# A fused adaLN, linear attention and gated MLP kernel: LayerNorm 1 transposes all on TensorE, query weights read transposed from DRAM, first key products in halves, and a new order of instructions

## The chip, the cores and the metric

The kernel runs on one core of a Trainium2 chip. The core has five engines with instruction queues of their own: TensorE (PE; its weight loads are listed as PEld), VectorE (DVE), ScalarE (ACT), GpSimd (POOL) and SyncE (SP), which here only issues DMAs. The metric is the time of one execution on the device in microseconds; three executions are known. A profiled execution gives times of single instructions, counted from the first one (the span).

## The reference

One token block of S = 2048 rows with D = 512, H = 32 heads of 16, F = 1376, in bfloat16. Cut to what matters:

```python
mod = (silu(c) @ w_mod)                      # six vectors sa, ca, ga, sb, cb, gb of 512
h = layernorm(x) * (1 + ca) + sa
q, k, v = heads(h @ wqkv)
pq, pk = q @ w_phi, k @ w_phi                # per head, 16 x 16
phi_q = concat(softmax(pq), softmax(-pq));   phi_k = concat(softmax(pk), softmax(-pk))
kv = phi_k.T @ v;  z = phi_k.sum(tokens)     # sums over all 2048 tokens
o = (phi_q @ kv) / (phi_q @ z + 1e-6)
x = x + ga * (o @ wo)
h = layernorm(x) * (1 + cb) + sb
x = x + gb * ((sigmoid(h @ w_gate) * (h @ w_up)) @ w_down)
```

The sums kv and z run over all tokens, so no token can pass the attention before all keys and values have been worked off.

## The kernel before

**Tiles.** The 2048 rows are 16 tiles of 128. `x_sb` holds them with rows on partitions. LayerNorm 1 works per tile: `st1` (statistics, DVE), `rs1` (one over the deviation, on ACT or POOL), `nmr1` (DVE), `xn1` (normalised rows, on POOL, ACT or, for tile 0, DVE). Then the rows must become columns, `h1T`, for the products. The groups `LG` are tiles 0, 1, 2-3, 4-5, ... 14-15. For a group with `TD` 0, PE transposes 128 x 128 blocks into a PSUM bank (`tph`, L841) and ACT or DVE applies the modulation on the way out (`hm1`, L848, L850). For groups 6 and 7 (tiles 10 to 13) `TD` is 1: SP issues a DMA transpose per tile straight into `h1T` (`xT1`, L833), and `hm1` changes `h1T` in place on ACT, DVE or POOL.

**Weights.** The head map `w_phi` is folded into the key and query weights: `bd` is its block-diagonal form, the weights are transposed (keys: `tpw` on PE and `wTc` copies; queries: `wqT`, DMA transposes from `wqk_sb` behind the load `wq0`, L769), multiplied (`fold`, L776) and copied to `wqk_f` (`foldc`, L782, L784). The modulation vectors are products of `wmod_sb` with silu(c), of one column each: `modc1` (LayerNorm 1; its two halves are the two halves of the contraction, loaded by `ld_wm00` and `ld_wm01`, L667), `modca` (ga) and `modc2` (the rest, in halves `modc2.0` and `modc2.1`), L735.

**Keys and values, per tile t.** `K` (four matmuls into `k_ps`, L867), `e` (exponentials of both signs, ACT, L883), `n` (sums, DVE, L886), `r` (reciprocal, DVE, or logarithm and exponential on ACT), `phi` (product, POOL or DVE, L889), `V` and its copy `va` (L907), and `kv` (eight matmuls per tile into two accumulating banks `kvacc`, L280). Tiles 11 and 13 to 15 do `e` to `kv` in parts (`NPART`). After the last tile, `kvm` masks the sums (DVE, L301), `kvp` permutes them (PE with `bdp`, which POOL's `perm` makes, L290, L293) and `kvz` and `kvn` write `kvbd`.

**Queries and the rest.** `Q` (L945) and `qe` (exponentials, L950) work on blocks of 128 features by 512 tokens, 16 in all. Behind `kvp` come, per unit of one or two tiles, `sm` or `num` (products with `kvbd`), divisions `den` and `u`, `o` and its transposition `oT`, `out` (with `wo`, which POOL and DVE scale by ga), `x1`, LayerNorm 2, and per chunk (1, 1, 2, 4, 4, 4 tiles) the MLP: `g`, `u`, the tanh `tg` on ACT, `hm`, `y` (L612), the addition `fin` (L619) and the store `st` (L621). The last tile's `y` is made in 384 and 128 columns.

**What sets the order.** Every step is a task with a name, the engines that it may run on, the keys that it reads and writes, and the buffers that it uses. The text `ORDER` lists all tasks; `arrange` walks it, takes the engine that a suffix names (`@A`, `@D`, `@P`) or else the first of the task's list, and gives buffers out first come, first served. Each engine executes its tasks in that order and waits where data or a buffer is not there. `warm` matmuls have no result that is used.

Of the kernel before, what the change touches and what calls it, by code (L numbers as in the profile page):

```python
# [49 lines left out]
K13 kv8.0 va10 e13.4 r11.2 ld_wu0 e13.0 phi9.0 n13.4 r11.4 r13.4 n13.0 e12.0 phi10.0 K15 Q11 ld_wd kv9.0 V14 phi11.0@D n12.0 e15.4 r13.0@A K14 kv10.0 phi11.2  # L50
phi11.4 phi11.6 e15.0 va13 Q03 Q01 e14.4 r12.0@A va14 e14.0 phi13.4@D phi13.0 phi12.0 n14.4 n14.0 r14.4@A r14.0 n15.0 n15.4 r15.4 phi14.4@D V12 kv11.4 Q13
modc2.0 va12 qe01 phi14.0 phi15.4@D qe13 r15.0@A kv11.0 kv11.6 kv11.2 gra kv12.0 V15 Q02 kv13.4 va15 qe03 phi15.0@D kv14.4 kv13.0 kv15.4 kv14.0 kvm1 kv15.0
Q32 kvm0 qe02 perm kvp2 kvp1 kvp0 kvz2 kvz1 kvz0 kvn0 modc2.1 sm0 sm2 qe32 modc2c kvn2@A kvn1@A wo2 smS2 smS0@D den0 den2 Q12 Q31 qe31 wo3 num00 qe11 num30
num01 Q30 num31 u00 u01 Q23 num20 u30 u31 qe12 u20 tpo0 num21 u21 oT0 wo1 wo0 wo_all sm1 smS1 o3 sm4 smS4 num10 out0 num11 den1 x1_0 qe30 qe23 Q33 Q21 Q22
num61 qe33 u11 st2_0 u10 o2 tpo1 rs2_0 gwb nmr2_0 den4 num70 u70 qe21 oT1 num71 xn2_0 u71 grb wd0 qe22 Q20 out1 wd10 xnT0 num60 x1_1 mod00 mod01 wd4 wd5 wd1
mod03 u60 qe20 mod02@A oT2 oT3 tsw u61 st2_1 out3 out2 u0.10 g0.10 tg0.10 u0.9 g0.9 tg0.9 g0.3 g0.0 wmod_free o7 hm0.10 oT7 hm0.9 wd2 rs2_1 g0.4 u0.0 o6 wd7
wr g0.6 tg0.0 tg0.4 x1_3 u0.4 hm0.0 hm0.4 oT6 nmr2_1 g0.2 u0.6 u0.3 u0.2 u0.8 tg0.6 tg0.3 g0.8 xn2_1 hm0.6 x1_2 sm3 hm0.3 tg0.2 tg0.8 xnT1 hm0.2 g0.1 hm0.8
mod13 mod12@A mod10@A tg0.1 st2_3 g0.7 u0.7 u0.1 tg0.7 mod11@A wd6 smS3 hm0.7 hm0.1 out7 g1.5 u0.5 g1.2 g0.5 tg1.2 tg0.5 u1.2 x1_7 g1.0 u1.5 g1.8 st2_2 hm0.5
hm1.2 g1.9 u1.10 u1.0 rs2_2 tg1.5 tg1.0 hm1.5 hm1.0 g1.10 u1.8 nmr2_2 tg1.10 tg1.8 hm1.10 hm1.8 u1.3 g1.1 g1.3 wd8 xn2_3@P wd3 u1.1 out6 xn2_2 tg1.1 tg1.3
den3 hm1.1 hm1.3 g1.4 g1.7 u1.4 y0.0 tg1.4 wd9 x1_6 hm1.4 y0.1 y0.2 g1.6 tg1.6 num40 y1.0 y0.3 u1.6 num50 y1.1 u1.9 tg1.9 st2_7 st2_6 rs2_4 hm1.6 xnT3 xnT2  # L60
y1.2 y1.3 num51 y0.4 tg1.7 num41 num81 hm1.9 u50 u40 u41 z81 num80 y0.5 y1.4 u1.7 hm1.7 u51 mod22@A z80 mod20@A mod23@P mod21@P num82 y1.5 y0.6 y0.7 nmr2_4
z82@D g2.2 o5 tg2.2 num90 y1.6 y1.7 y0.8 o4 xn2_7@P dn8 u800 u820 y0.9 y0.10 g2.1 tg2.1 y1.8 y1.9 u2.1 g2.4 u2.2 fin0 u811 hm2.2 u821 o8 oT5 oT4 g2.10 y1.10
u2.10 num92 num91 hm2.1 fin1 z91@D tg2.10 tg2.4 u2.4 hm2.10 hm2.4 z90 xn2_6 out4 g2.8 z92 tg2.8 dn9 st0 u2.0 u2.8 g2.5 x1_4 u921 u911 hm2.8 out5 u900 u920
x1_5 u2.5 num100 oT8 z100 tg2.5 o9 hm2.5 st2_4 g2.7 g2.0 tg2.7 xnT7 tg2.0 hm2.0 st2_5 u2.3 g2.3 xnT6 out8 u2.9 u2.7 rs2_3 tg2.3 hm2.3 x1_8 hm2.7 nmr2_3 st2_8
xn2_5@P oT9 g2.6 g2.9 tg2.6 tg2.9 num102 y3.0 u2.6 y3.1 y3.2 num101 y3.3 y3.4 y3.5 num111 hm2.9 z101@D hm2.6 y3.6 mod42@A y3.7 y3.8 y3.9 z102 dn10 y3.10 fin3
xn2_4@P u1000 y2.0 y2.1 y2.2 out9 mod41@P num110 y2.3 x1_9 u1021 z110@D st2_9 xnT5 xnT4 y2.4 st3 y2.5 mod40@A y2.6 y2.7 y2.8 mod31@P mod43@A z111 mod33@P
# [1067 lines left out]
```

## Time and profile before

| | us |
|---|---|
| runs of the kernel | 208.19, 208.26, 208.80 (median 208.26) |
| the profiled execution, its own time | 208.63 |
| its span, first to last instruction | 206.9 |
| mean granted TensorE clock | 0.999 |
| PE busy | 199.4 (96%) |
| DVE, ACT, POOL busy | 168.8, 110.1, 96.3 |

The page gives busy time per engine, the span in 40 slices, DMA queues, the chain that ended last, and the costliest groups of instructions. Behind it stand the views that the prediction uses: busy time in chosen stretches, the waits by engine, the chain in order of time, groups by line and shape, and the timeline. In a group's row the columns are: line, engine, operation, what is written from what, shapes and count, busy time and mean length in ns of one, idle time just before them and who ended it. "L841" is line 841 of the kernel. Some records of matmuls are missing, so counts in a row can be a few below the program's.

### The profile page before, as it was taken

What the parts mean: (1) busy time and instruction counts of PE and PEld (TensorE: products, weight loads), DVE (VectorE), ACT (ScalarE), POOL (GpSimd) and SP (SyncE); (2) the same over time, 40 slices, a digit from 0 to 9 for tenths busy, and PEclk for the clock granted to TensorE, in tenths of its full rate; (3) what the DMA queues carried; (4) which work ended last, traced back from release to release, by engine and by line L of the source; (5) the groups of instructions that cost most, each with busy time, mean ns of one, the idle gap of its engine ahead of it and who ended that gap; (6) DMA issues with size and microseconds to landing.
All of it is one profiled execution on the core that took longest, in us unless ns stands there. A gap on an engine that the chain in (4) does not pass through costs nothing.

```text
span 206.9 us, 4373 instructions
## 1 busy us (share of the span) xinstructions
PE 199.4 (96%) x1539; PEld 112.8 (54%) x1563; DVE 168.8 (82%) x462; ACT 110.1 (53%) x267; POOL 96.3 (47%) x128
## 2 busy tenths in 40 slices
PE   7889999999999999999999999999999999999993
PEld 2465554554676689768764544454444444444442
DVE  3999999998989998999999999898797865235632
ACT  2689999999979986433343543231523351144100
POOL 5787999999976987774256000014400220000000
PEclk9999999999999999999999999999999999999999
DMA  6999877697101211205321121141223022000111
GB/s 161 341 351 237 106 194 261 183 382 242 55 0 54 51 32 25 54 0 103 72 49 34 39 42 25 26 91 39 52 51 76 5 51 76 0 0 29 33 52 54
DMA packets 32557, 19.27 MB, mean 93 GB/s; under 512 B 21169, under 2 KB 30738, under 8 KB 32530
## 3 DMA queue, kind: packets, MB, share of 16 engines
q1 hardware_dynamic: 32000, 18.92, 34.3%
q8 instruction: 14, 0.23, 0.5%
q14 instruction: 13, 0.11, 0.2%
q10 hardware_dynamic: 530, 0.02, 0.1%
HBM read 12.11 MB, written 2.10 MB: 69 GB/s over the span
## 4 chain that ended last, share of the span: by engine, by line
PE 71%; ACT 18%; DMA 4%; DVE 3%; SPq 2%; issue 1%; DVEq 0%; ACTq 0%
PE y_ps L612 18%; PE u_ps L574 17%; PE g_ps L574 17%; ACT e L883 8%; PE a_ps L483 7%; PE q_ps L945 4%; ACT h1T L848 4%; DMA wmod_sb<-in_w_mod_dram 4%; ACT vaug L907 3%; PE num L366 2%; PE num L450 2%; DVE phi L889 1%; PE g_ps L576 1%; SPq L664 1%; DVE ks L886 1%
## 5 line engine op out<-in xcount | busy, mean ns | idle before, releaser
L584 ACT ACTIVATE tg<-g_ps 128x512 bf16<-128x512 f32 (+5 forms) x66 | 28.9, 454 | 58.0 <-PE g_ps L574 38.1
L612 PE MATMUL y_ps<-wd_sb,wmod_sb 128*128 128x512 bf16 (+4 forms) x184 | 43.8, 366 | 0.2
L595 DVE SCALAR_TENSOR_TENSOR wmod_sb<-tg,u_ps 128x512 bf16<-128x512 bf16 (+4 forms) x63 | 30.0, 494 | 15.0 <-ACT tg L584 7.3
L574 PEld LDWEIGHTS <-wu_sb 128*128 128x128 bf16 (+1 forms) x252 | 21.7, 99 | 15.7 <-issue 0.2
L574 PEld LDWEIGHTS <-wg_sb 128*128 128x128 bf16 (+1 forms) x252 | 21.5, 99 | 14.7 <-issue 0.2
L889 POOL TENSOR_TENSOR phi<-e,ks 128x1024 bf16<-128x1024 bf16 (+2 forms) x17 | 27.7, 1637 | 1.1 <-DVE ks L899 0.3
L612 PEld LDWEIGHTS <-wmod_sb 128*128 128x128 bf16 (+1 forms) x187 | 17.4, 98 | 16.9 <-issue 0.2
L574 PE MATMUL u_ps<-wT_sb,wu_sb 128*128 128x512 bf16 (+2 forms) x122 | 23.7, 321 | 0.1
L574 PE MATMUL g_ps<-wT_sb,wg_sb 128*128 128x512 bf16 (+2 forms) x122 | 23.7, 321 | 0.1
L503 POOL TENSOR_SCALAR ve<-mv 128x2 f32<-128x2 f32 (+1 forms) x8 | 1.8, 223 | 42.3 <-DVE mv L493 42.3
L574 PE MATMUL u_ps<-wqk_sb,wu_sb 128*128 128x128 bf16 (+4 forms) x127 | 19.9, 287 | 0.1
L886 DVE TENSOR_REDUCE ks<-e 128x64 f32<-128x1024 bf16 (+2 forms) x22 | 19.7, 903 | 0.3 <-ACT e L883 0.2
L574 PE MATMUL g_ps<-wqk_sb,wg_sb 128*128 128x128 bf16 (+4 forms) x127 | 19.6, 287 | 0.1
L883 ACT ACTIVATE e<-k_ps 128x512 bf16<-128x512 f32 (+2 forms) x44 | 18.4, 500 | 0.0
L950 ACT ACTIVATE eT<-q_ps 128x512 bf16<-128x512 f32 x32 | 16.8, 611 | 1.8 <-PE q_ps L945 1.7
L474 POOL TENSOR_TENSOR o<-u 128x512 bf16<-128x512 f32 x10 | 12.6, 1269 | 9.5 <-DVE u L456 4.2
L619 DVE TENSOR_TENSOR ot<-y_ps,x 128x512 bf16<-128x512 f32 (+2 forms) x17 | 11.2, 656 | 6.9 <-PE y_ps L612 6.6
L483 PE MATMUL a_ps<-wo_sb,oT 128*128 128x512 bf16 x57 | 15.7, 379 | 0.4
L945 PE MATMUL q_ps<-h1T,wqk_f 128*128 128x512 bf16 x62 | 15.7, 379 | 0.1
L867 PE MATMUL k_ps<-wqk_f,h1T 128*128 128x512 bf16 x63 | 15.5, 379 | 0.1
L871 PE MATMUL v_ps<-wv_sb,h1T 128*128 128x512 bf16 x59 | 15.2, 379 | 0.2
L799 DVE BATCH_NORM_STATS2 st<-x_sb 128x6 f32<-128x512 bf16 x16 | 10.8, 673 | 2.6 <-DMA x_sb<-in_A_x_dram 2.6
(156 smaller groups left out, 334.7 us busy)
## 6 DMA issues: line engine op xcount, KB each, us to landing
out_dram<-ot SPq DMA_DIRECT2D x15, 128.0 KB, 1.8
x_sb<-in_A_x_dram SPq DMA_DIRECT2D x6, 256.0 KB, 5.0
wmod_sb<-in_w_mod_dram SPq DMA_DIRECT2D x3, 512.0 KB, 6.5
wmod_sb<-in_w_mod_dram SPq DMA_DIRECT2D x1, 1536.0 KB, 10.3
wg_sb<-in_B_w_gate_dram SPq DMA_DIRECT2D x1, 1376.0 KB, 7.1
wd_sb<-in_B_w_down_dram SPq DMA_DIRECT2D x1, 1280.0 KB, 13.9
wu_sb<-in_B_w_up_dram SPq DMA_DIRECT2D x1, 768.0 KB, 11.0
wu_sb<-in_B_w_up_dram SPq DMA_DIRECT2D x1, 608.0 KB
```

The lines of the kernel that those rows point to most:

```text
L483: pe.matmul(ap_[:], lhsT=oT[:, j, :], rhs=wo_sb[:, j, :], start=(j == 0), stop=(j == KT - 1))
L574: pe.matmul(ps[:fsz, 0:n], lhsT=w[:, j, ft * P:ft * P + fsz], rhs=h[:, j, 0:n], start=(j == 0), stop=(j == KT - 1))
L584: G.add(f"tg{k}.{ft}", {"ACT": 0.13 + n * 0.00083}, lambda e, tg=tg, g_ps=g_ps, fsz=fsz, n=n: act.activation(tg[:fsz, 0:n], g_ps[:fsz, 0:n ...
L595: dve.scalar_tensor_tensor(hm_all[:fsz, hm[k].slot, ft, 0:n], tg[:fsz, 0:n], 1.0, u_ps[:fsz, 0:n], op0=ALU.add, op1=ALU.mult)
L612: mm = pe.matmul(y[:, 0:c1 - c0], lhsT=hm_all[:fsz, hm[k].slot, ft, tl * P:(tl + 1) * P], rhs=wd_sb[:fsz, ft, c0:c1], start=(ft == 0), sto ...
L867: pe.matmul(kp[:], lhsT=h1T[:, j, t * P:(t + 1) * P], rhs=wqk_f[:, j, D:2 * D], start=(j == 0), stop=(j == KT - 1))
L871: pe.matmul(vp[:], lhsT=h1T[:, j, t * P:(t + 1) * P], rhs=wv_sb[:, j, :], start=(j == 0), stop=(j == KT - 1))
L883: act.activation(ee[:, ha:hb, s, :], kp[:, ha * DH:hb * DH].rearrange("p (h j) -> p h j", j=DH), ACT.Exp, scale=1.0 - 2.0 * s)
L886: dve.tensor_reduce(ks[:, ha:hb].rearrange("p h s -> p (h s)"), ee[:, ha:hb].rearrange("p h s j -> p (h s) j"), axis=AX.X, op=ALU.add)
L889: engine(e).tensor_tensor(ph[:, ha * 32:hb * 32].rearrange("p (h j) -> p h j", j=DH), ee[:, ha:hb].rearrange("p h s j -> p (h s) j"), ks[: ...
L945: pe.matmul(qp[:], lhsT=wqk_f[:, j, blk * P:(blk + 1) * P], rhs=h1T[:, j, cq * 512:(cq + 1) * 512], start=(j == 0), stop=(j == KT - 1))
L950: act.activation(eT[cq][:, s * 4 + blk, :], qp[:], ACT.Exp, scale=1.0 - 2.0 * s)
```

## The change

- **LayerNorm 1 transposes.** `TD` is 0 for all groups: the four DMA transposes `xT1` go, and tiles 10 to 13 get eight `tph` tasks of two transposes each on PE; their `hm1` reads PSUM and runs on ACT or DVE.
- **Query weights.** `DIRECT[0]`: the load `wq0` goes; the four DMA transposes `wqT` read `A_wqkv` in DRAM and depend on nothing. The half of `wqk_sb` that the load filled now takes the ga weights (`wga_sb`).
- **Key weights.** The two loads are cut by rows instead of columns, so that their rows in DRAM are 1 KiB instead of 512 bytes. `tpw` transposes one row block, its copy is spread over `wT_sb`, and `fold` waits for one copy instead of four.
- **Modulation 1.** Four loads of 256 columns (512-byte rows) instead of two of 1024 (2 KiB rows); `modc1` becomes two tasks, by output blocks 0-1 and 2-3, each with a copy of its own, and `hm1` waits for its half only.
- **Halves.** `K` for tiles 0 to 7 and `V` for tiles 0 to 3 are two tasks of two matmuls each, which wait for half of the h1 blocks (and of the folded or value weights). `wv`, `wg` and `x3` are loaded in two parts.
- **VectorE.** `xn1` (but for tile 0) may run on POOL or ACT, POOL by default; no `hm1` reads and writes SBUF on DVE; `phi` may be on DVE only from tile 13 on.
- **Warm matmuls.** 12 single ones instead of 16.
- **Order.** A new `ORDER` for everything. Ahead of `kvp` stand six query blocks instead of eight, and all of `modc2` instead of its first half. `rs1_1` is on POOL. The last tile's `y` ends with the 384 columns instead of the 128.

```diff
-TD = [0, 0, 0, 0, 0, 0, 1, 1, 0]
+TD = [0, 0, 0, 0, 0, 0, 0, 0, 0]
+KSP = 8
+DIRECT = [1, 0]
+VSP = 4
-SPLIT = {"wk": 2, "wv": 1, "wq": 1, "wg": 1, "wu": 2, "x1": 2, "x2": 2, "x3": 1}
+SPLIT = {"wk": 2, "wv": 2, "wq": 2, "wg": 2, "wu": 2, "x1": 2, "x2": 2, "x3": 2}
...
+wdz warm0 c1 ld_x0b st1_2 st1_3 warm1_0 warm1_1 warm1_2 warm1_3 warm1_4 pmem ld_x0a c2 st1_0 bd c3 st1_1 ld_wk1 tpw3 rs1_1@P rs1_2 warm1_5 tpw2 rs1_0 wTc3
+wTc2 xn1_0 nmr1_2 ld_wk0 tpw1 tpw0 warm1_6 wTc1 wTc0 ld_x1a warm1_7 fold12 fold11 fold13 tph01 ld_x2a ld_wm00b foldc12 foldc11 st1_4 fold10 warm1_8 warm1_9
+warm1_10 st1_9 nmr1_1 ld_wm00a st1_5 st1_8 warm1_11 foldc10 foldc13 modc1.0 xn1_3 xn1_2 ld_wm01b ld_wm01a tph00 tph20 tph22 ld_x2b xn1_1 tph10 tph12 tph21
+modc1c0 hm1_20@A hm1_21 hm1_00 hm1_01@A hm1_10@A modc1.1 modc1c1@D rs1_3@P nmr1_3 K2a tph13 tph11 hm1_13 K0a st1_11 hm1_22@A hm1_11@A tph03 tph23 tph02 K3a
+ld_wv0 rs1_5@P hm1_03 xn1_4 xn1_5 hm1_23@A hm1_12@A V1a K2b hm1_02@A nmr1_5 ld_x1b xn1_9 xn1_8 st1_10 K3b ld_x3b st1_6 st1_7 ld_wv1 wqT0 K0b e2.0 e0.0 tph30
...
+kv13.4 kv13.0 kv14.0 kv14.4 kv15.4 Q01 kvm1 qe02 qe12 kv15.0 kvm0 grb ld_wd2 wd0 Q32 gwa gra wo1 wo3 qe01 kvp0 kvp1 kvp2 kvn0 kvz1 kvz0 kvz2 Q10 wo0 wd2 wo2
...
+y15.9b y15.10b fin15b st15b y15.1 y15.2 y15.3 y15.4 y15.5 y15.6 y15.7 y15.8 y15.9 y15.10 fin15 st15
...
     def load_wm(i):
-        load(f"wm0{i}", [("wmod0", i)], lambda e: sp.dma_start(wmod_sb[:, 2 * i:2 * i + 2, 0:1024], wmod_v[:, 2 * i:2 * i + 2, 0:1024]), 512 * K1)
+        for s in range(2):
+            c = s * D + 256 * i
+            load(f"wm0{i}{'ab'[s]}", [("wmod0", i, s)], lambda e, c=c: sp.dma_start(wmod_sb[:, :, c:c + 256], wmod_v[:, :, c:c + 256]), 256 * K1)
...
+    def modc1_task(h):
+        ps = bank("modc_ps", [P, 2, 2])
+        dst = modc[:, 0:8].rearrange("p (s j) -> p s j", s=2)[:, :, 2 * h:2 * h + 2]
...
+        G.add(f"modc1.{h}", {"PE": 0.4}, f, r=[("wmod0", h, 0), ("wmod0", h, 1), "scbf"], w=[("mc1ps", h)], bufs=[ps])
+        G.add(f"modc1c{h}", {"ACT": 0.35, "DVE": 0.15}, f2, r=[("mc1ps", h)], w=[("mod1", h)], bufs=[ps])
...
+                if DIRECT[0]:
+                    G.add(f"wqT{k}", {"SP": 1.2}, lambda e, k=k: sp.dma_start_transpose(wT_sb[:, 0, :, k * P:(k + 1) * P], A_wqkv[k * P:(k + 1) * P, 0:D]),
+                          w=[("wT", 0, k)], nbytes=-1)
...
-            G.add(f"fold{side}{kt_in}", {"PE": 0.24}, f3, r=[("wT", side, k) for k in range(KT)] + ["bd"], w=[("fold", side, kt_in)], bufs=[ps])
+            G.add(f"fold{side}{kt_in}", {"PE": 0.24}, f3, r=[("wT", side, kt_in), "bd"], w=[("fold", side, kt_in)], bufs=[ps])
...
-                w = {"DVE": 0.171 + 0.035 * n, "ACT": 0.25 + 0.11 * n, "POOL": 0.12 + 0.165 * n}
-                G.add(f"hm1_{g}{j}", w, f_m, r=[("h1raw", t) for t in ts] + ["mod1"],
+                w = {"ACT": 0.25 + 0.11 * n, "POOL": 0.12 + 0.165 * n}
+                G.add(f"hm1_{g}{j}", w, f_m, r=[("h1raw", t) for t in ts] + [("mod1", j // 2)],
...
+        if t < KSP:
+            for h in range(2):
+                js = (2 * h, 2 * h + 1)
+                G.add(f"K{t}{'ab'[h]}", {"PE": 0.435}, lambda e, js=js, f=f_k: f(e, js), r=[h1k[j] for j in js] + [("wqk", j, 1) for j in js], w=[("k", t)], bufs=[kp])
```

More of the change, by code (lines that the diff above doesn't have):

```diff
@@ L51 @@
[L51 to L54, printed above, removed]
@@ L643, in f_b @@
             dve.tensor_reduce(bst[:, 2:3], bsq[:, 4:8], axis=AX.X, op=ALU.add)
-        G.add("bndb", {"DVE": 1.2}, f_b, r=[("bnd", j) for j in range(KT)] + ["mod1"], w=["bst"])
+        G.add("bndb", {"DVE": 1.2}, f_b, r=[("bnd", j) for j in range(KT)] + [("mod1", 0), ("mod1", 1)], w=["bst"])
         ps = bank("bnd", [1, 3])
@@ L722 @@
     warm("warm0", 6, 2.4, r=["wdz"], w=["warm"])
-    for i in range(16):
+    for i in range(12):
         warm(f"warm1_{i}", 1, 0.22, r=["c1"], w=["warm"])
@@ L828, in f_xn @@
                     pool.tensor_scalar(xn[:], x_sb[:, t, :], rs1[:, t:t + 1], nmr[:, 0, t:t + 1], op0=ALU.mult, op1=ALU.add)
[L829 removed]
+            G.add(f"xn1_{t}", {"POOL": 0.69, "ACT": 0.73} if t else {"DVE": 0.3}, f_xn, r=[("rs1", g)] + ([("nmr1", g)] if t else []), w=[("xn1", t)],
                   bufs=[xn], port=("POOL", "DVE"))
```

159 lines of the change are left out of this document (89 added, 70 removed).

## The prediction

> **What bounds the kernel now.** I read the page first, then busy time in three stretches that I cut where the program changes character, then TensorE's (PE's) waits, then the chain of waits in order of time. The three stretches are: until the first key product K2 loads its weights (13.26), from there to the products `kvp` that close the sum over all keys (56.93), and from there to the end of the last matmul (203.71). Columns: stretch, its length, then busy us (instructions) of PE, its weight loads, DVE, ACT and POOL, clock, DMA share, GB/s.
>
> ```profile
> 0.00:13.26 13.26, 10.75 (x103) 5.91 (x103) 9.05 (x29) 7.40 (x19) 8.81 (x31) 1.00 0.87 276
> 13.26:56.93 43.67, 42.75 (x373) 23.78 (x380) 41.66 (x88) 42.85 (x110) 41.22 (x40) 1.00 0.79 214
> 56.93:203.71 146.78, 145.87 (x1065) 83.07 (x1080) 117.83 (x345) 59.83 (x139) 46.29 (x59) 1.00 0.18 42
> ```
>
> In the middle stretch all four engines are over 94% busy; behind it only PE is (145.87 of 146.78). A busy PE need not be a full one, so I look at what it waits for, and at the chain.
>
> ```profile
> ...
> PE modc_ps L735 <- DMA wmod_sb<-in_w_mod_dram: 0.5, 1, 0.5
> PE kvacc L280 <- POOL phi L889: 0.3, 1, 0.3
> PE kvacc L280 <- DVE phi L889: 0.2, 1, 0.2
> ```
>
> Only 0.5 us of PE's waits lie behind the first key. The chain (start, length, what):
>
> ```profile
> 4.45 7.29 DMA wmod_sb<-in_w_mod_dram
> ...
> 11.79 0.57 PE modc_ps L735 x16
> ...
> 12.65 3.19 ACT h1T L848 x8
> 15.83 2.92 ACT e L883 x6
> ...
> 50.00 0.57 ACT e L883 x2
> ...
> 56.23 0.86 PE q_ps L945 x4
> 57.10 0.50 PE kvp L316 x16
> 57.60 0.66 PE modc_ps L735 x24
> ```
>
> The start hangs on the modulation weights, which land at 4.45 + 7.29 = 11.74. The chain then runs through ACT, nearly without a gap, to the last exponential at 50.6, through a string of DVE steps, and into PE. A matmul of 512 columns takes 0.216 (four in 0.86). The middle stretch holds 64 key, 64 value and 32 query matmuls of that size, 34.6 us, and 128 small `kvacc` ones, 35 transposes, 16 folds and 40 modulation matmuls that fill most of the rest: PE has at most 43.67 - 42.75 = 0.92 us to give. So the end is: first key, plus PE's work, plus 206.9 - 203.7 = 3.2 us of tail. I sum against that.
>
> **The change, part by part.**
>
> *Earlier start.* Modulation weights come in four DMAs by output columns, so that the first half (`modc1.0`, `modc1c0`) serves h1 blocks 0 and 1, and K2 is cut so that K2a needs only these. But PE's queue holds `modc1.1` ahead of K2a, and that needs the second half. Ahead of it stand the same 2.5 MiB as before (x0, x1a, x2a, key weights, modulation weights); what differs is the length of the rows: 512 bytes where 2 KiB were, and 1 KiB where the key weights had 512 bytes.
>
> ```profile
> 5.00:6.00 1.00, 1.00 (x6) 0.48 (x5) 0.93 (x4) 0.50 (x2) 0.00 (x0) 1.00 1.01 299
> 6.00:7.00 1.00, 0.49 (x3) 0.00 (x0) 0.96 (x5) 0.50 (x2) 0.48 (x1) 1.00 1.09 297
> 9.00:10.00 1.00, 1.00 (x8) 0.53 (x7) 0.91 (x3) 1.00 (x3) 0.92 (x3) 1.00 1.00 371
> 10.00:11.00 1.00, 1.00 (x27) 1.00 (x25) 0.93 (x4) 0.95 (x4) 0.93 (x2) 1.00 1.06 390
> 13.00:14.00 1.00, 0.89 (x9) 0.51 (x8) 1.00 (x6) 1.00 (x4) 1.00 (x3) 1.00 1.10 348
> ```
>
> By bytes in issue order the key weights move at 5 to 7 (298 GB/s), the modulation weights at 8 to 11 (380), the value weights with 1 KiB rows at 13 (348). So 1.05 MB go from 2.76 to 3.52 us (+0.76) and 0.52 MB from 1.76 to 1.51 (-0.25): landing at 12.25, ends 11.5 and 12.5. With 0.05 + 0.57 for `modc1.1`, K2a starts at 12.87, 0.4 before 13.26 (ends 1.15 and 0.15). I take the middle, because both kinds of rows have a rate of their own above. The Trainium skill speaks against the cut: "Perfetto Trace Analysis", DMA Optimizations, says that small DMAs, under 2 KB, carry a significant overhead per transfer. Without it the landing would be 11.5 and the forecast 0.75 lower; the 298 against 380 GB/s agree with it.
>
> ACT is not later: it makes eight copies (four `wTc`, four `foldc`) before the first h1 block, instead of seven with `foldc12` on DVE, at 0.53 each (two in 1.07, below), but the third DMA now brings key weights, not the fourth: 7.50, less 0.75 for one 256 KiB load at 350 GB/s, plus eight times 0.53, is 11.0, and some 11.25 with the two small copies of `modc1c0`.
>
> ```profile
> 7.50 1.07 ACT L763 COPY wT_sb<-tp_w 128x512 bf16<-128x512 bf16 x2 [0.81 <-PE tp_w L759]
> 13.26 0.33 PEld L867 LDWEIGHTS <-h1T 128*128 128x128 bf16 x3
> 16.38 5.29 SPq L769 DMA_TRANSPOSE wT_sb<-wqk_sb  x4
> 19.07 0.39 PE L841 MATMUL tp_h<-ident,xn 128*128 128x128 bf16 x4
> 21.56 7.94 POOL L889 TENSOR_TENSOR phi<-e,ks 128x1024 bf16<-128x1024 bf16 x4
> 23.60 1.06 PE L776 MATMUL fold_ps<-bd,wT_sb 128*128 128x128 bf16 x16
> 53.80 0.53 POOL L290 MEMSET bdp<- 128x512 bf16 x1
> 54.39 1.76 POOL L293 COPY bdp<-ident 128x64 bf16<-128x64 bf16 x4
> ```
>
> *Transposes.* Tiles 10 to 13 go to PE: 16 transposes more. Three others slip behind the first key (10 instead of 13 stand before it), so 19 more lie in the full stretch. One costs (0.39 - 0.22) / 3 = 0.057 us, 0.22 being the length of a single one (its row stands with POOL's, below): **+1.1**. I charge them in full, as PE has no idle to take them. Four DMA transposes leave SP's queue, where they had waited for their rows.
>
> *Query weights from DRAM.* One 512 KiB load and the wait for it go; four transposes read DRAM. None reads DRAM in this trace; four from SBUF held SP for 5.3 us (16.38 to 21.7), 1.3 each, and their readers ran at 23.60. Now they wait for nothing and are issued some 5 us sooner, while the first reader, `fold03`, stands later, behind `kv0.0`: 0, covered by about 7 us. Taking twice as long (10.6 us) they would be just in time; beyond that PE waits one for one, and a saving is impossible, as nobody waited for them. Behind them on SP stand x3a, `wu1` and the later weights, none wanted before 20 us.
>
> *What moves across `kvp`.* Eight query blocks stood before it, now six; the 24 `modc2.1` matmuls (0.66) go ahead of it. PE's sum is the same: `kvp` at 56.93 - 0.4 + 1.1 - 1.73 + 0.66 = 56.55, and 146.78 + 1.73 - 0.66 = 147.85 behind it.
>
> *Cover for 56.55.* ACT up to the last exponential: two h1 blocks (0.40 each: eight in 3.19), two reciprocals, one `rs1` and the mod2 copies (short pairs, some 0.4 each) more, one xn (0.7) and one query pair (two of 0.49: six in 2.92) less, +0.7: 50.9 with the start term's 0.4, and only four DVE steps, 2.4 us, behind it. DVE loses a fold copy, one reciprocal and a quarter of phi, about 1.1. POOL is the tight one:
>
> ```profile
> L841 PE MATMUL tp_h<-ident,xn 128*128 128x128 bf16 x48 | 5.0, 219 | 0.0
> L828 POOL TENSOR_SCALAR xn<-x_sb,rs,nmr 128x512 bf16<-128x512 bf16 x13 | 9.9, 768 | 3.0 <-ACT ve L806 2.9
> L889 POOL TENSOR_TENSOR phi<-e,ks 128x1024 bf16<-128x1024 bf16 x12 | 23.1, 1927 | 0.9 <-DVE ks L899 0.3
> L889 DVE TENSOR_TENSOR phi<-e,ks x5: 424/693/1311, 47.0 to 55.2; 128x512 bf16<-128x512 bf16 x4, 128x256 bf16<-128x256 bf16 x1
> ```
>
> From its first phi on it has one xn (0.77) and a quarter phi (0.7) more, two h1 blocks (1.1) and one `rs1` (0.9) less: -0.6. But `rs1_1` moves to it ahead of all xn, and `nmr1_4`, which its last two xn wait for, stands on DVE behind the 1.2 us sum `n0.0`: I put its first phi between 21.6 and 22.5. `perm` (53.80 to 56.15) then ends between 55.5 and 56.5, just under 56.55. I add nothing.
>
> *Smaller.* Halved keys and values keep their matmuls: 0. `V1a` stands on PE ahead of K2b and wants the value weights, which land near 13.9 by the same rates, while PE gets to it near 14.2: 0, at worst 0.3, and K2b, then e2, wait behind it. That spends PE's hoped-for share of its 0.5 us of waits; I leave the sum alone.
>
> *Tail.* The last output tile ended with its 128 columns; now it ends with the 384.
>
> ```profile
> L619 DVE TENSOR_TENSOR ot<-y_ps,x 128x384 bf16<-128x384 f32 x1 | 0.6, 558 | 1.1 <-PE y_ps L612 1.1
> L619 DVE TENSOR_TENSOR ot<-y_ps,x 128x128 bf16<-128x128 f32 x1 | 0.3, 291 | 0.1
> out_dram<-ot SPq DMA_DIRECT2D x1, 96.0 KB, 2.1
> out_dram<-ot SPq DMA_DIRECT2D x1, 32.0 KB, 1.8
> ```
>
> 0.56 for 0.29 and 2.1 for 1.8: **+0.6**.
>
> **Sum:** -0.4 + 1.1 + 0.6 = +1.3 on a span of 206.9. The profiled execution took 208.63 and the median of the runs is 208.26; on the median that is 209.5, slower by 0.6%. About 0.3%, 0.6 us, is what a measurement here can tell from no change.
>
> **Rivals.**
> *Faster: ACT's chain, not PE, sets `kvp`.* ACT's first h1 block needs only the first half of the modulation weights, and could start near 11.25 instead of 12.65; with +0.7 of work the last exponential ends at 49.9, `kvp` follows near 53.7 (the four DVE steps, the last `kvacc` and its masking), and the end is 53.7 + 147.85 + 3.8 = 205.3, 1.6 less: 206.7. For it speaks the chain, which is ACT's for 35 us; against it PE's 42.75 of 43.67. It decides the sign once `kvp` starts before 55.3, and is measurable before 54.7.
> *No change: the weights land in time.* Landing at 11.5 gives -1.15, and half of PE's 0.9 us of idle closes: -1.15 + 1.1 + 0.6 - 0.5 = 0, 208.3. For it: the overlap of row lengths at 7 to 9 us blurs my rates.
> *Much slower: DVE and POOL block each other over phi.* DVE's half phi takes 0.69 alone and took 1.31 next to one of POOL's. One of four did so; now DVE's `phi13.4`, `phi14.0` and `phi15.4` run while POOL has phi 12, 13 and 14 without a break. Two to three more of 0.62 push POOL's `perm` and DVE's last phi to about 57.8: 210.8. The Trainium skill, "SBUF — State Buffer", SBUF: two separate sides, calls the shared port pair an exclusive lock that fully blocks the loser; 1.31 against 0.69 agrees. Stalls that the new order makes behind `kvp`, where any is added to the end, belong here too.
>
> **How the numbers follow.** Forecast 0.47 (209.5, its own range 208.9 to 210.3), much slower 0.18, no change 0.19, faster 0.16. The range of 8 in 10 leaves out most of the faster case and the far end of added stalls: 207.6 to 211.8. Slower by over 0.3%: 0.65; within: 0.19; faster: 0.16.
>
> **What would show it.** K2a's weight load at 12.9 (start term), with a PE wait for the modulation weights before it; 64 `tp_h` transposes instead of 48 and `kvp` at 56.5 (transpose term); PE over 99% busy behind it for 147.9 us; the last DVE step 0.56 long and the end 3.8 after the last matmul. I am wrong if `kvp` comes before 55.3, if PE has more than 1 us of new waits anywhere, or if the transposes from DRAM keep `fold03` waiting.

## The result, and the profile after

The changed kernel takes 210.32 us (median of four executions, 209.71 to 211.75), the kernel before 208.22 beside it: ratio 1.0107, 95% interval 1.0075 to 1.0139. It is slower by 2.1 us; I had forecast 209.5, slower by 1.2. The profiled execution took 209.71 and its span is 208.0, 1.1 longer than the 206.9 of before. It was the quickest of the four, so the sums below are made against it, and the missing 0.6 to 1 us is looked for afterwards.

The first view is busy time in three stretches, cut as in the prediction: until the weight load of the first key product, from there to the first product `kvp`, from there to the end of the last matmul (columns as there).

```profile
0.00:12.19 12.19, 10.28 (x95) 5.58 (x96) 8.22 (x26) 7.71 (x19) 8.32 (x33) 1.00 0.90 261
12.19:55.68 43.49, 43.18 (x421) 24.64 (x418) 41.55 (x88) 41.40 (x113) 41.48 (x40) 1.00 0.70 207
55.68:204.81 149.13, 148.65 (x1066) 83.12 (x1064) 115.41 (x340) 59.06 (x137) 54.42 (x68) 1.00 0.17 39
```

Against the rows of before the first stretch is 1.07 shorter (13.26), the second 0.18 shorter (43.67), the third 2.35 longer (146.78). From the last matmul to the end of the span it is 3.2 us in both (208.0 - 204.81; 206.9 - 203.71). Sum: +1.1. My forecast of the same four was -0.4, 0, +1.07 and +0.6: a sum of +1.3 that came out nearly right by luck, from terms of which three were wrong by 0.6 or more.

The chain of waits (start, length, what) has in part changed hands. Where ACT's exponentials carried it for 35 us, DVE now carries it from 12.9 to 23.4 and PE from 25.5 to 44.9. The 8.7 us from there to the last `kvacc` products are again ACT's last exponentials and then DVE's steps, as in the kernel before.

```profile
5.47 6.29 DMA wmod_sb<-in_w_mod_dram
11.80 0.55 PE modc_ps L759 x16
...
23.54 1.94 POOL phi L926
25.52 0.43 PE kvacc L287 x8
...
26.60 0.86 PE v_ps L903 x4
...
44.93 1.13 ACT e L920 x4
...
52.76 0.88 DVE phi L926
...
55.85 0.50 PE kvp L323 x16
...
204.85 0.56 DVE ot L626
```

The modulation weights still land at 5.47 + 6.29 = 11.76 (before: 11.74), but the first key follows 0.43 behind, not 1.5. Before, ACT made the first h1 block only behind this landing (at 12.65 in the chain before); now blocks 0 and 1 need only the first half of these weights, ACT begins them ahead of the landing, and only `modc1.1` stands between it and the first key. ACT's timeline shows it:

```profile
11.07 1.26 ACT L880 ACTIVATE h1T<-tp_h,modc 128x256 bf16<-128x256 bf16 x3
```

`fold03` waits for nothing. PE's waits (what waited, for whom, us in total, times, longest):

```profile
...
PE modc_ps L759 <- DMA wmod_sb<-in_w_mod_dram: 0.6, 1, 0.6
PE u_ps L581 <- DVE wmod_sb L602: 0.2, 1, 0.2
PE kvacc L287 <- DVE phi L926: 0.2, 1, 0.2
PE g_ps L581 <- DVE x L495: 0.2, 1, 0.2
```

Two of these are new and lie behind `kvp`. They look small, but a wait is counted from the modelled end of the matmul before it, and that end lies late: a group of four is listed with 0.39, while the next one starts 0.22 behind it. So I count from start to start. PE's timeline (start, length, instructions) shows what the waits cost:

```profile
75.96 0.61 PE L581 MATMUL g_ps<-wqk_sb,wg_sb 128*128 128x128 bf16 x8
76.41 0.39 PE L581 MATMUL u_ps<-wqk_sb,wu_sb 128*128 128x128 bf16 x4
77.04 0.61 PE L581 MATMUL u_ps<-wqk_sb,wu_sb 128*128 128x128 bf16 x8 [0.24 <-DVE wmod_sb L602]
...
83.52 0.40 PE L457 MATMUL num<-kvbd,eT 128*128 128x128 bf16 x4
84.11 0.38 PE L581 MATMUL g_ps<-wT_sb,wg_sb 128*128 128x128 bf16 x4 [0.20 <-DVE x L495]
```

Eight products start 0.45 before the next group (75.96 to 76.41), so four take 0.22; from 76.41 to 77.04 it is 0.63, so 0.41 is lost and not 0.24, and 0.37 from 83.52 to 84.11. Worked out in this way over all matmuls of 75 to 85 us, PE loses 1.3 us there. That is the part of the third stretch that the forecast lacks: 2.35 = 1.07 of moved work + 1.3.

### The profile page after: what moved, and what is told of

It is laid out like the page before. It is cut to its first block, busy times and chain, and to the rows that moved or that the text cites. A ratio compares the mean times of both kernels' runs of the same rounds, so it can differ in the third digit from the quotient of the medians.

```text
span 208.0 us, 4402 instructions
## 1 busy us (share of the span) xinstructions
PE 202.1 (97%) x1575; PEld 113.4 (55%) x1575; DVE 165.7 (80%) x455; ACT 108.2 (52%) x267; POOL 104.2 (50%) x139
## 4 chain that ended last, share of the span: by engine, by line
PE 79%; DVE 9%; DMA 3%; ACT 3%; SPq 2%; POOL 2%; issue 1%; POOLq 0%; DVEq 0%
PE y_ps L619 18%; PE g_ps L581 17%; PE u_ps L581 17%; PE a_ps L490 6%; PE q_ps L987 5%; PE k_ps L899 3%; DMA wmod_sb<-in_w_mod_dram 3%; PE v_ps L903 3%; DVE ks L923 2%; PE num L373 2%; ACT e L920 2%; PE num L457 2%; PE g_ps L583 1%; PE kvacc L287 1%; DVE st L831 1%
## 5 line engine op out<-in xcount | busy, mean ns | idle before, releaser
L619 PE MATMUL y_ps<-wd_sb,wmod_sb 128*128 128x512 bf16 (+4 forms) x187 | 44.8, 367 | 0.0
L926 POOL TENSOR_TENSOR phi<-e,ks 128x1024 bf16<-128x1024 bf16 (+2 forms) x18 | 28.4, 1592 | 1.2 <-ACT ks L934 0.4
L481 POOL TENSOR_TENSOR o<-u 128x512 bf16<-128x512 f32 x13 | 16.4, 1271 | 19.0 <-DVE u L448 10.9
L899 PE MATMUL k_ps<-wqk_f,h1T 128*128 128x512 bf16 x64 | 16.7, 379 | 0.0
L903 PE MATMUL v_ps<-wv_sb,h1T 128*128 128x512 bf16 x64 | 16.4, 379 | 0.0
L490 PE MATMUL a_ps<-wo_sb,oT 128*128 128x512 bf16 x64 | 16.3, 379 | 0.0
```

What stands on the lines that cost most here:

```text
L490: pe.matmul(ap_[:], lhsT=oT[:, j, :], rhs=wo_sb[:, j, :], start=(j == 0), stop=(j == KT - 1))
L619: mm = pe.matmul(y[:, 0:c1 - c0], lhsT=hm_all[:fsz, hm[k].slot, ft, tl * P:(tl + 1) * P], rhs=wd_sb[:fsz, ft, c0:c1], start=(ft == 0), sto ...
L899: pe.matmul(kp[:], lhsT=h1T[:, j, t * P:(t + 1) * P], rhs=wqk_f[:, j, D:2 * D], start=(j == 0), stop=(j == KT - 1))
L903: pe.matmul(vp[:], lhsT=h1T[:, j, t * P:(t + 1) * P], rhs=wv_sb[:, j, :], start=(j == 0), stop=(j == KT - 1))
L926: engine(e).tensor_tensor(ph[:, ha * 32:hb * 32].rearrange("p (h j) -> p h j", j=DH), ee[:, ha:hb].rearrange("p h s j -> p (h s) j"), ks[: ...
```

## The experiments

Each is the changed kernel, or where it is said another experiment, with the edit shown. All were timed against the kernel before on the same chip (its medians 208.3 to 208.5). The table is worked out from the traces of the profiled executions: landing of the second load of key weights and of the last modulation weights for the first norm, start of the first key's weight load, length of the second and third stretch (bounds as above), span; then the median time.

```
                          keys   mod.   first  first key  kvp to       span   median
                          land   land   key    to kvp     last matmul
before                    7.84   11.74  13.26  43.67      146.77       206.9  208.22
after                     6.66   11.76  12.19  43.49      149.13       208.0  210.32
a_dma_transposes          7.15   12.28  12.72  48.78      148.66       214.1  215.58
a2_dma_transposes_act     6.66   11.74  12.18  47.96      148.84       212.5  216.01
a3_dma_transposes_late    6.34   11.44  12.28  49.03      148.84       213.6  214.89
b_long_rows               7.02   11.45  12.76  43.50      148.99       208.5  210.27
c_whole_keys              6.72   11.84  12.58  43.97      149.12       209.3  211.03
d_tail_order              6.83   11.92  12.35  43.51      149.13       208.0  210.26
e_stalls_75_85            7.58   12.69  13.13  45.17      148.51       210.2  209.41
f_warm_cover              7.21   12.33  12.76  43.51      149.13       208.6  210.09
g_query_weights_sbuf      7.32   12.43  12.87  44.42      149.13       210.3  212.19
h_double_transposes       7.40   12.54  12.97  44.18      149.12       209.5  210.96
i_stalls_and_warm         6.76   11.87  12.39  43.49      148.19       207.6  209.29
j_early_modulation        7.73   12.03  13.19  46.12      148.17       210.7  212.15
```

**The transposes, priced by doubling (h_double_transposes).** On top of f_warm_cover, below.

```diff
-                for tl, xn in enumerate(xns):
+                for tl, xn in enumerate(xns * (2 if g in (6, 7) else 1)):
+                    tl = tl % len(xns)
                     pe.transpose(tp[:, tl * P:(tl + 1) * P], xn[:, j * P:(j + 1) * P], ident[:])
```

> The kernel of f_warm_cover with each of the 16 transposes of tiles 10 to 13 done twice into the same place, the result unchanged: 16 more on TensorE and nothing else. My transpose term says that TensorE has no idle time to take them: 16 x 0.057 = 0.9, so kvp and the end come 0.9 later than in f_warm_cover, median 211.0. Rival, ACT and VectorE set kvp: 0 to 0.3 later, median 210.1 to 210.4.

The median is 210.96, 0.87 over f_warm_cover (ratio to before 1.0142, 1.0104 to 1.0180). The middle stretches of f_warm_cover and of this kernel:

```profile
12.76:56.27 43.51, 42.75 (x414) 24.62 (x418) 41.56 (x88) 41.26 (x112) 41.13 (x40) 1.00 0.71 205
```
```profile
12.97:57.15 44.18, 43.95 (x438) 25.50 (x435) 41.48 (x88) 41.38 (x112) 40.90 (x39) 1.00 0.69 197
```

It is 0.67 longer for 16 transposes, 0.042 each; the rest of the 0.87 is the first key, 0.2 later in this profile. From start to start a transpose still takes 0.056, 0.9 for 16; the difference is mostly two of PE's waits for phi, which shrank from 0.25 to 0.14 and from 0.15 to 0.07. DVE, ACT and POOL, 41 us busy of 44, did not absorb the rest. So the theory holds for the part that the doubling tests: all these transposes lie ahead of 45.4, up to there PE sets the pace, and 19 more of them cost 0.8 at this rate (I had 1.1). Behind the last key products the chain to `kvp` runs through ACT and DVE here too, unchanged; whether more work of PE there would move `kvp` was not tested.

**The same transposes taken away (three tries).** Tiles 10 to 13 go back to DMA transposes. The first try leaves the modulation steps on their engines:

```diff
-TD = [0, 0, 0, 0, 0, 0, 0, 0, 0]
+TD = [0, 0, 0, 0, 0, 0, 1, 1, 0]
-                w = {"ACT": 0.25 + 0.11 * n, "POOL": 0.12 + 0.165 * n}
+                w = {"ACT": 0.25 + 0.11 * n, "POOL": 0.12 + 0.165 * n, "DVE": 0.171 + 0.035 * n}
 ORDER: tph60..63, tph70..73 out; xT1_10 xT1_11 behind ld_wmm2, hm1_60@D behind hm1_40, xT1_12 xT1_13 behind xn1_13
```

> The changed kernel, but tiles 10 to 13 are transposed by DMA again (16 transposes less on TensorE). My transpose term: TensorE is full between the first key and kvp, so kvp moves from 55.85 to 54.95 (16 x 0.057 = 0.9 us earlier), the end of the span follows: 207.1 where the changed kernel's profiled span was 208.0. Rival, the other engines set kvp (ACT, DVE and POOL are busy 41.7 to 41.8 of the 43.7 us): kvp no earlier than 55.5, span 207.7 or more, and TensorE shows the 0.9 us as waits.

Neither: 215.58 (ratio 1.0349, 1.0322 to 1.0375), the middle stretch 5.3 longer. Some 1.6 of that is a fall of the clock to 0.5 between 13 and 17, as under *The clock* below. The new operations in the trace, first DVE's steps that read SBUF (times in ns: shortest, median, longest), then DVE's timeline, then POOL's:

```profile
L885 DVE TENSOR_SCALAR h1T<-h1T,modc x4: 346/858/2099, 27.1 to 44.3; 128x256 bf16<-128x256 bf16 x4
```
```profile
35.90 2.10 DVE L885 TENSOR_SCALAR h1T<-h1T,modc 128x256 bf16<-128x256 bf16 x1
...
38.73 1.27 DVE L885 TENSOR_SCALAR h1T<-h1T,modc 128x256 bf16<-128x256 bf16 x1
```
```profile
35.98 3.94 POOL L929 TENSOR_TENSOR phi<-e,ks 128x1024 bf16<-128x1024 bf16 x2
```

A step of 0.35 took 2.10 and another 1.27. POOL ran two phi from 35.98 to 39.92, 1.94 each, the first to 37.92; the DVE steps end at 38.00 and 40.00, each 0.08 behind the end of a phi. They were held for as long as the phi ran. The step of 0.45 at 44.26 also ends 0.08 behind the end of a phi (44.62), and the one of 0.35 began only 0.13 before such an end. "SBUF — State Buffer" of the Trainium skill, SBUF: two separate sides, says that the shared ports are locked for a whole instruction and the loser fully blocks; this trace agrees. In the kernel before three such steps ran while POOL had no phi, and took 0.33 to 0.48.

The second try puts the steps on ACT and those of tiles 12 and 13 later; the third, on top of f_warm_cover, also moves the first one:

```diff
 a2: hm1_60, 61, 62, 63, 70, 71, 72, 73 all @A; hm1_42, 43, 53, 82 on DVE; hm1_70, 72 behind e10.0, hm1_71, 73 behind r9.0
 a3: as a2, but hm1_60@A behind e6.0; hm1_72 behind r9.0, hm1_71, 73 behind e11.0
```

> The changed kernel with tiles 10 to 13 transposed by DMA, as in a_dma_transposes, but mended in two ways: the eight modulation steps that read the transposed tiles from SBUF are all on ACT (four steps that ACT did from accumulators go to VectorE instead), and those of tiles 12 and 13 stand later, so that nobody waits for the DMA. In a_dma_transposes one such VectorE step took 2.1 us where 0.35 is its shortest; if that collision with POOL's phi and the wait for the DMA made the loss of 6 us, this kernel loses both. My transpose term then gives kvp 0.9 earlier than the changed kernel with the same start (55.85 less 0.9 = 54.95; a late start adds to it) and a median near 209.4. Rival, ACT and VectorE are as full as TensorE, so that the transposes cost nothing that could be given back: kvp within 0.3 of the changed kernel, median near 210.3.

> The kernel of f_warm_cover with tiles 10 to 13 transposed by DMA and modulated on ACT, as in a2_dma_transposes_act, but with the first modulation step of tiles 10 and 11 behind e6.0: in a2 ACT waited 2.9 us for the landing at 27.0 and everything behind it was late. If that one wait made the loss, the kernel comes back to within 1 us of f_warm_cover, and if the transposes cost TensorE what I said, 0.9 under it (median 209.2). Rival, the loss is in the load of ACT and VectorE, which the SBUF reads and the shifted steps do not lighten: median 211 or more.

They took 216.01 (1.0354, 1.0310 to 1.0399) and 214.89 (1.0300, 1.0272 to 1.0328). In a2 ACT waits for a landing, in a3 PE waits for the modulation steps that I had put too late:

```profile
27.00 0.60 ACT L883 ACTIVATE h1T<-h1T,modc 128x256 bf16<-128x256 bf16 x1 [2.93 <-DMA h1T<-xn]
```
```profile
PE v_ps L906 <- ACT h1T L883: 2.5, 2, 1.7
```

My theory for a3 falls: the one wait was not the whole loss. What these three show is the price of a misplaced step in an order written by hand. Whether a good place would give back the 0.7 that the doubling measured stays open.

**The gaps at 75 to 85 (e_stalls_75_85, i_stalls_and_warm).**

```diff
-... tg0.7 tg0.6 st2_2 smS3 xn2_1 u0.7 g0.2 u0.6 hm0.7 hm0.6 tg0.2 ...
+... tg0.7 tg0.6 smS3 xn2_1 u0.7 g0.2 u0.6 hm0.7 hm0.6 st2_2 tg0.2 ...
-... o6@D hm0.5 ... rs2_2 nmr2_2 ... hm0.10 den3 x1_7 ...
+... o6 hm0.5 den3 ... rs2_2 nmr2_2 ... hm0.10 x1_7 ...
 i: also the four warming products of f_warm_cover, and st2_2 between hm0.7 and hm0.6
```

> The changed kernel, but three VectorE and POOL steps are moved in the order: the statistics st2_2 behind hm0.7 and hm0.6, the reciprocal block den3 from behind nmr2_2 to ahead of it, and o6 to POOL. If TensorE's start-to-start gaps between 75 and 85 us (1.3 us in sum, of which 0.8 near 77 and 0.5 near 84) come from VectorE being late with the steps that free accumulators, they fall to under 0.5 and the end comes 0.8 to 1.3 earlier: span 206.7 to 207.2. Rival, the gaps come from the many short products with too few accumulators and no order of VectorE changes it: gaps stay above 1.0, span 207.8 to 208.2.

> The kernel of f_warm_cover with the moved steps of e_stalls_75_85, but st2_2 now between hm0.7 and hm0.6: in e_stalls_75_85 a gap of 0.56 was left at 79.9, just behind st2_2. If the gaps at 75 to 85 us are VectorE's lateness, nearly all of their 1.3 us go: behind kvp 147.7 us of TensorE instead of 148.9, median 208.8 to 209.0. Rival, they only wander: median 209.4 as in e_stalls_75_85. In both cases it stays slower than the kernel before by 0.3 to 0.9.

e takes 209.41 (1.0055, 1.0033 to 1.0077), i takes 209.29 (1.0046, 1.0032 to 1.0060). The third stretch of i has the same instructions on PE as that of the changed kernel and is 0.94 shorter:

```profile
55.88:204.07 148.19, 148.05 (x1066) 82.91 (x1064) 114.86 (x339) 59.01 (x137) 55.15 (x69) 1.00 0.17 39
```

0.39 of the 1.3 us is left, as a gap of 0.30 at 77 and one of 0.09 at 79. So the gaps come from the order: between short products of four matmuls, each of which wants an accumulator back, DVE did statistics (0.87) and a block of reciprocals (1.4) ahead of the steps that give accumulators back. The edit puts the statistics behind them, the reciprocals ahead, where DVE had been idle for 0.70, and `o6` (0.69) on POOL; the three were not told apart. In time the gain is 0.8 to 0.9; i misses my 208.8 to 209.0 by 0.3. It is the best version that I ran, and the kernel before stays 0.3 to 0.6% ahead.

**The tail (d_tail_order).** The names of the two parts of the last tile are swapped in ORDER (`y15.*` with `y15.*b`, and so their `fin` and `st`).

> The changed kernel, but the last output tile ends with its 128 columns and not with the 384, as before the change. My tail term: 0.27 for the last VectorE step and 0.3 for the landing, so the span falls from 208.0 to 207.4, with 2.6 us less or so between last matmul and end only by those two. Rival, read from the trace after (3.2 us from the last matmul to the end in both kernels): the last store lands as fast as it is the last, whatever its size, and the gain is 0.0 to 0.3, which can't be told from nothing.

210.26 (1.0090, 1.0069 to 1.0112), where the changed kernel has 210.32 (1.0107, 1.0075 to 1.0139): no difference. Store landings of the changed kernel and of this one (KB each, median us from issue to landing):

```profile
out_dram<-ot SPq DMA_DIRECT2D x1, 96.0 KB, 1.6
out_dram<-ot SPq DMA_DIRECT2D x1, 32.0 KB, 2.1
```
```profile
out_dram<-ot SPq DMA_DIRECT2D x1, 96.0 KB, 1.7
out_dram<-ot SPq DMA_DIRECT2D x1, 32.0 KB, 1.5
```

The store that is issued last lands in 1.6 with 96 KB and in 1.5 with 32 KB (1.8 in the kernel before); the 2.1 that I had read as the price of 96 KB is no matter of size. The stretch from the last matmul to the end is itself no fixed quantity: in the profiles of the twelve kernels that end with the 384 columns it is 3.2 to 3.9 with the same last steps.

**The start: rows, halves, query weights.** Long rows:

```diff
-        for s in range(2):
-            c = s * D + 256 * i
-            load(f"wm0{i}{'ab'[s]}", ..., wmod_sb[:, :, c:c + 256], ...)
+        load(f"wm0{i}", ..., wmod_sb[:, 2 * i:2 * i + 2, 0:2 * D], ...)
 ORDER: ld_wm00 and ld_wm01 where the four loads stood, modc1.0 behind tph21
```

> The changed kernel, but its modulation weights come in two DMAs with 2 KiB rows instead of four with 512-byte rows, at the same places of the queue; both halves of the products then wait for the second. My start term priced the short rows at 0.75 us: the last of these weights would land at 11.0 instead of 11.76. Rival, rows of 512 bytes move as fast as longer ones and only bytes count: landing stays within 0.15 of 11.76. In the second case the first key waits for both halves in a row and starts 0.5 to 1.0 later than 12.19, and the end is later by as much (span 208.5 to 209.0); in the first it starts at about 12.2 and the span stays at 208.0.

210.27 (1.0094, 1.0077 to 1.0111). DMA rates from 8 to 11 us, the changed kernel first (last column GB/s):

```profile
8.00:9.00 1.00, 0.91 (x14) 0.73 (x14) 0.96 (x3) 1.00 (x3) 1.00 (x2) 1.00 1.20 311
9.00:10.00 1.00, 1.00 (x12) 0.54 (x9) 0.97 (x4) 1.00 (x3) 1.00 (x3) 1.00 1.21 289
10.00:11.00 1.00, 1.00 (x26) 0.95 (x25) 0.96 (x3) 1.00 (x4) 0.96 (x3) 1.00 1.18 301
```
```profile
8.00:9.00 1.00, 1.00 (x17) 0.84 (x16) 0.97 (x4) 1.00 (x3) 1.00 (x2) 1.00 1.05 395
9.00:10.00 1.00, 1.00 (x9) 0.45 (x6) 0.96 (x4) 1.00 (x3) 1.00 (x2) 1.00 1.01 381
10.00:11.00 1.00, 0.63 (x8) 0.32 (x7) 0.96 (x3) 0.71 (x2) 1.00 (x3) 1.00 1.08 375
```

The short rows cost what I said: 300 GB/s for 380, and the landing comes 5.10 behind the key weights in the changed kernel and 4.43 in this one, 0.67 apart (I had 0.75; "Perfetto Trace Analysis" of the Trainium skill, DMA Optimizations, gives no size for its overhead of small DMAs). The edit also makes two loads of four; row length and number of loads are not told apart. In the change this price and the two halves cancel: with long rows the weights land sooner, the first key follows 1.31 behind them instead of 0.43, and the time is the same.

Undivided products:

```diff
-KSP = 8
-VSP = 4
+KSP = 0
+VSP = 0
 ORDER: K0a..K7a, V0a..V3a out
```

> The changed kernel with undivided keys and values (the first key product waits for all four h1 blocks of its tile and so for both halves of the modulation weights). TensorE has the first halves of K2, K0, K3 and V1 (8 x 0.216 = 1.7 us) to do before 13.9 in the changed kernel and would stand idle instead. If it is full from there on, the end is 1.7 later (median 212.0), and as much again (213 to 214) if the idle time makes the granted clock fall to 0.5 for three microseconds, as it did in the profiles of e_stalls_75_85 and a_dma_transposes. Rival, the chain of exponentials on ACT sets the pace and the halves only fill time: 0.3 later (210.6).

211.03 (1.0119, 1.0098 to 1.0140), 0.7 more, between the two theories; the intervals overlap (1.0075 to 1.0139 without this edit), but the trace shows 0.8: the first key follows 0.74 behind the landing instead of 0.43, and the middle stretch is 0.48 longer. The first key did not wait for 13.9: its first matmul needs one h1 block and starts at 12.58, and PE then waits inside the product:

```profile
PE k_ps L901 <- ACT h1T L882: 0.6, 2, 0.4
```

Query weights through SBUF, as before the change:

```diff
-DIRECT = [1, 0]
+DIRECT = [0, 0]
-    wga_sb = wqk_sb[:, :, 0:D]
+    wga_sb = wmod_sb[:, :, 2 * D:3 * D]
 ORDER: ld_wq0 ld_wq1 where wqT0 stood, wqT0 behind ld_x3a
```

> The changed kernel with the query weights loaded to SBUF and transposed from there, as before the change. My prediction gives the transposes from DRAM no effect, since about 7 us cover them: median within 0.3 of 210.3, kvp within 0.2 of where the start puts it, and no wait of TensorE at fold03. Rival, 512 KiB more in SP's queue ahead of x3a delay the later tiles: xn of tiles 12 to 15 later, POOL's phi stream with gaps, median above 210.8.

212.19 (1.0190, 1.0166 to 1.0215), not equal, and not by the rival's way either. A wait for later weights is new on PE, and a transfer on the chain of waits goes with it:

```profile
PE modc_ps L748 <- DMA wmod_sb<-in_w_mod_dram: 0.8, 1, 0.8
```
```profile
23.50 9.80 DMA wmod_sb<-in_w_mod_dram
...
33.35 0.70 PE modc_ps L748 x16
```

SP stands before the four transposes until the query weights land, the ga weights behind them are issued at 23.5 instead of 18.0, and `modca` (the 16 products) waits for them. 0.9 of the loss is this (44.42 for 43.51). Another 0.7 of the span lies behind the last matmul: 3.9 us, but a_dma_transposes has 3.9 and c_whole_keys 3.6 there with the same last steps, so it need not belong to this edit; its cause stays open.

An earlier landing, on top of i:

```diff
-... ld_x2a ld_wm00b ... st1_4 fold10 ... st1_9 nmr1_1 ... st1_8 ... ld_wm01b ld_wm01a ...
+... ld_wm00b ... st1_4 fold10 ... nmr1_1 ... ld_wm01b ld_wm01a ld_x2a ... hm1_13 st1_9 ... hm1_03 st1_8 ...
 rs1_5 behind xn1_5; nmr1_5 xn1_9 xn1_8 behind st1_10
```

> The kernel of i_stalls_and_warm with one load moved: x2a (256 KiB, tiles 8 and 9) behind the four loads of modulation weights instead of ahead of them, and the statistics of these tiles behind the first key. If the landing of these weights sets the first key, as in my start term, they land 0.7 earlier and kvp and the end come 0.3 to 0.7 earlier (ACT's fold copies end at 10.9 and may hold the first h1 block): median 208.2 to 208.6. Rival, VectorE's two statistics (1.7 us) now stand between the first h1 steps and delay the keys behind them: kvp later, median 209.3 or more.

212.15 (1.0181, 1.0162 to 1.0200). The weights land 4.30 behind the key weights instead of 5.10, but the first key is no sooner (5.46 behind them, 5.53 in the changed kernel): PE's warming products ahead of `modc1.0` run to 11.1, so this does not test the landing. The late statistics then starve POOL, and PE with it:

```profile
POOL ve L844 <- DVE mv L835: 1.7, 1, 1.7
```
```profile
PE tp_h L876 <- POOL xn L863: 2.1, 2, 1.8
```

**The clock (f_warm_cover).** The profile of e_stalls_75_85 was its slowest execution, 211.9 where the other six took 209.1 to 210.3. Its waits and its windows from 12 to 17 us (the granted clock stands ahead of the last two columns):

```profile
PE modc_ps L762 <- ACT h1T L883: 0.7, 1, 0.7
PE modc_ps L762 <- DMA wmod_sb<-in_w_mod_dram: 0.5, 1, 0.5
```
```profile
12.00:13.00 1.00, 0.29 (x11) 0.27 (x11) 0.66 (x2) 1.00 (x3) 0.92 (x3) 1.00 1.11 349
13.00:14.00 1.00, 1.00 (x17) 0.60 (x14) 0.40 (x3) 0.54 (x2) 0.35 (x2) 0.68 1.09 346
14.00:15.00 1.00, 1.00 (x6) 0.45 (x5) 0.87 (x2) 0.55 (x2) 1.00 (x2) 0.50 2.09 281
15.00:16.00 1.00, 1.00 (x7) 0.58 (x5) 0.96 (x6) 0.59 (x2) 0.30 (x2) 0.50 0.65 65
16.00:17.00 1.00, 1.00 (x4) 0.40 (x3) 0.96 (x3) 0.68 (x2) 1.00 (x2) 0.61 1.03 282
```

The modulation weights landed at 12.69, PE idled 0.5 and 0.7 us, and then the clock fell to 0.5 for some 3.4 us. The second stretch is 1.7 longer (45.17). a_dma_transposes shows the same: idle for 0.39 and 0.71 at 10.2 and 11.6, then a clock of 0.5 to 0.6 from 13 to 16. But idling of this length does not always bring the fall. In g_query_weights_sbuf PE had the same two waits (0.43 and 0.70, at 10.3 and 11.8), and the clock stayed at 1.00:

```profile
PE modc_ps L762 <- ACT h1T L883: 0.7, 1, 0.7
PE modc_ps L762 <- DMA wmod_sb<-in_w_mod_dram: 0.4, 1, 0.4
```
```profile
13.00:14.00 1.00, 0.95 (x10) 0.54 (x8) 0.83 (x5) 0.74 (x2) 0.54 (x1) 1.00 1.11 350
14.00:15.00 1.00, 1.00 (x9) 0.53 (x8) 0.96 (x4) 0.94 (x3) 0.98 (x2) 1.00 1.10 345
```

What else decides is open. The changed kernel's execution of 211.75 has the same mean clock, 0.992, as this one; without a trace of it that is a likeness, not a proof.

```diff
-    for i in range(12):
+    for i in range(16):
 ORDER: warm1_12 warm1_13 ahead of modc1.0, warm1_14 warm1_15 ahead of modc1.1
```

> The changed kernel with four more warming products (0.22 each): two ahead of modc1.0 and two ahead of modc1.1, in the places where TensorE waits for the modulation weights. The waits there were 0.58 in the profile of the changed kernel (granted clock 1.0 after) and 0.46 + 0.71 in that of e_stalls_75_85 (granted clock 0.5 to 0.7 from 13 to 16.7, and the key products at half speed). If idle time there makes the clock fall, no execution of this kernel shows a mean clock under 0.995 and its slowest is within 0.5% of its fastest, where the changed kernel had one of four at 211.75; the median stays within 0.3 of 210.3. Rival, the clock falls for another reason: some execution shows 0.992 again.

210.09 (1.0079, 1.0063 to 1.0095): 209.97 to 210.46, no mean clock below 0.998, though its weights landed late (12.33). With h, i and j, which have the same products, that is twenty-one executions with no mean clock below 0.997 (one of h took 213.09 at full clock, for a reason that no trace shows). Without the products the changed kernel, d and e had two of 0.992 in seventeen, g two in five (0.992 and 0.989), b and c none in ten, and a and a2 ten in twelve. a3 has the products too and shows 0.983 to 0.992 in five of six; in its profile the clock falls at 42 to 50, behind waits of 0.8 and 1.7 us at 41 and 43. This speaks for the theory without settling it.

## Why the prediction was right in its sum and wrong in its terms

- *Earlier start*, -0.4: -1.07 in this execution, -0.7 on average over the six profiles with an unchanged start (after, a, a2, d, e, g), where the first key begins at 12.57. The mechanism was right, and so were the price of the short rows (0.67 for 0.75) and the landing, forecast at 12.25 and 12.14 on that average. The step that failed is the one behind the landing: I gave `modc1.1` 0.05 + 0.57, and the first key's weight load follows after 0.43 to 0.44 in all six, because it begins before the modelled end of the last product. The rest of the -1.07 is an early landing in this one execution: the key weights landed at 6.66 here, between 6.34 and 7.73 in the thirteen profiles that load them at the same place, and what is behind them in the queue moves along. The kernel before has one profile only, so its 13.26 may be early or late in the same way.
- *Transposes*, +1.1: 0.8 by the doubling. There are 64, as foreseen, and 0.056 each was right; what I left out is that PE's waits for phi give way. The first `kvp` stands at 55.68 for 56.55, of which 0.68 is the start and 0.19 the middle.
- *Query weights from DRAM*, 0: no wait at `fold03`, as said. That the DRAM form also brings the loads behind it on SP forward, the ga weights for `modca` by 5.5 us, I did not see; undone in this order, it costs 0.9 at least.
- *What moves across `kvp`*, 0 in sum, +1.07 behind it: right, and exact to 0.02 once the gaps are taken out.
- *Smaller* ("Halved keys and values keep their matmuls: 0"): the halves are worth 0.8 by the trace, of which part is the start.
- *Tail*, +0.6: 0. The DVE step took 0.56, as foreseen; the landing was mis-read by size (1.6 for the 2.1 of the sum).
- *Stalls behind `kvp`*, none in the sum: +1.3. This is the step that failed by most. I had named them, put them with the much slower rival, and given PE "over 99% busy" as their test. PE is 99.7% busy by that row and 1.3 us short all the same. My other sign, more than 1 us of new waits on PE, shows it only when counted from start to start; the view of waits gives 0.4.
- *Rivals.* DVE and POOL over phi: DVE's four half phi took 0.69 to 1.02, no worse than before (0.69 to 1.31), and POOL's `perm` is not on the chain. ACT's chain: it no longer carries the stretch up to 44.9, and doubling PE's transposes there moved `kvp`; behind that it still does.

On the median I was 0.8 too low, at the upper edge of the forecast's own range. The profiled execution had an early landing; a first key at 12.76 and the rest as here make a span of 208.6, as in f_warm_cover, and two of the three executions not profiled have just that span. It fits, but no trace of them shows it.

## What to carry to other kernels

Where a profile shows an engine over 99% busy, count the starts of its instructions: waits counted from a modelled end showed 0.4 of 1.3 us here, and a good part of the new order's price lay in them. Price a disputed operation by doing it twice in place; taking it away moved three engines and told little. In an order written by hand, a step costs where it stands and not what it takes: a 0.35 us step cost 2.1, and a landing in front of the wrong one 2.9.

## What the hardware showed that I had not expected

- Two idle stretches of 0.5 and 0.7 us, with only transposes and one-column products around them, and the granted clock fell to 0.5 for 3.4 us, 1.7 us of time (e_stalls_75_85; with 0.39 and 0.71 also a_dma_transposes). "TensorE: Matmul & The Clock Gate" of the Trainium skill, Why this matters for your kernels, asks only for no idle gaps over some 3 us between bursts; in these two traces shorter ones went ahead of a fall. In a third, g_query_weights_sbuf, 0.43 and 0.70 did not, so the condition is not found.
- The same loads in the same order landed up to 1.4 us apart from one profile to the next (key weights, 6.34 to 7.73), and the first key followed the modulation weights behind them by 0.43 or 0.44 in eight of them.
- DMA rows of 512 bytes moved at 300 GB/s and rows of 2 KiB at 380, in the same place of the same queue (four loads of 256 KiB against two of 512).
